# One hand-laid SBUF tile for two alternating transformer layers, and new orders of work at their seams

## The chip, the cores and the metric

The kernel runs on one core of a Trainium2 chip. The metric is device time in microseconds. The core has five engines with instruction streams of their own: TensorE (PE, with its weight loads shown apart as PEld), VectorE (DVE), ScalarE (ACT), GpSimd (POOL) and SyncE (SP); transfers are issued by SP, ACT or POOL and carried out by 16 DMA engines. On-chip data lie in SBUF, and PE writes its sums to PSUM.

## The reference

Four residual layers, A, B, A, B, over 2048 rows of 640 values in bfloat16. Both A layers have the same weights, and so have both B layers.

```python
x = x + A(layernorm(x));  x = x + B(layernorm(x))
x = x + A(layernorm(x));  x = x + B(layernorm(x))

def A(x, mem0, Wq, Wk, Wv, Wo, seg_len):      # 32 heads of 192, seg_len 32
    mem = mem0                                # 8 memory rows
    for s in range(64):
        h = concatenate([mem, x[32*s : 32*s+32]])
        q, k, v = h @ Wq, h @ Wk, h @ Wv      # per head
        p = softmax(where(mask, q @ k.T * scale, -1e9))
        o = (p @ v) @ Wo
        mem = o[:8]                           # the recurrence
        outs.append(o[8:])

def B(x, wqkv, w_phi, wo):                    # 32 heads of 20, linear attention
    q, k, v = split(x @ wqkv)
    phi_q = [softmax(q @ w_phi), softmax(-q @ w_phi)]
    phi_k = [softmax(k @ w_phi), softmax(-k @ w_phi)]
    kv, z = phi_k.T @ v, phi_k.sum(rows)
    return (phi_q @ kv) / (phi_q @ z + 1e-6) @ wo
```

Layer A is sequential: a segment needs the memory rows of the one before. The last 8 rows of every segment aren't needed by the next one, so the kernel computes them apart, in a preparation and a closing stage with large matmuls.

## The kernel before

A layer A consists of `A_pre` (queries, keys and values of the last 8 rows of every segment, in two halves of 32 segments and four rounds of 8 heads), `A_chain` (the recurrence) and `A_post` (the output product of those last rows). Weights of layer A stay in SBUF but for nine pieces, `wslot`, that are loaded anew in every segment, as is one part of `Wo`.

```python
with tc.tile_pool(name=f"A{li}_wres", bufs=1) as wres:
    big = wres.tile([P, NRES * PW], BF16, name="w_res")      # resident weights, rounds 3, 0, 1, 2
    slot = {(m, b): wres.tile([P, PW], BF16, name=f"wslot{m}{b}") for ...}
    wo_mid = wres.tile([P, 24 * 640], BF16, name="wo_mid")
    wo_end = wres.tile([P, 12 * 640], BF16, name="wo_end")
    ...
    self.A_pre(...)
    self.A_chain(...)
    self.A_post(at_dram, li, wo_mid, wo_end, big)
```

The closing stage, four blocks of 16 segments: tails are fetched, reordered by copies on DVE and ACT in turn, multiplied, and stored in 16 pieces.

```python
def A_post(self, at_dram, li, wo_mid, wo_end, big):
    ...
    for tb in range(NSEG // 16):
        o = 7680 + 12288 * (tb % 3)
        ot = big[:, o:o + 6144]...
        nc.sync.dma_start(out=ot, in_=self.otb_d[16 * tb:16 * tb + 16]...)
        ow = big[:, o + 6144:o + 12288]...
        for k in range(4):
            self.ev.copy(out=ow[:, 12 * k:12 * k + 12, :]..., in_=ot[:, :, 96 * k:96 * k + 96]...)
        for c in range(48):
            nc.tensor.matmul(p0[:, :], lhsT=ow[:, c, :], rhs=w[:, 0:512], ...)
            nc.tensor.matmul(p1[:, 0:128], lhsT=ow[:, c, :], rhs=w[:, 512:640], ...)
        ob = ...                                    # one copy on DVE, one on ACT
        for s in range(16):
            dq.next().dma_start(out=at_dram[row:row + 8, :], in_=ob[8 * s:8 * s + 8, :])
```

Layer B has pools of its own. It loads its weights and builds constants, then works in two phases over four groups of 512 rows.

```python
with tc.tile_pool(name=f"B{li}_w", bufs=1) as wp, ...:          # x2, wqkv, wo, wbd, osum, zm, expd, phi
    for j in (1, 2, 0):
        nc.scalar.dma_start(out=wqkv[:, :, D * j:D * j + D], in_=...)
    ...                                                        # constants on POOL: wbd, blk, mask, osum, expd

    def norm_T(g):                                             # four blocks of 128 rows
        for b in range(4 * g, 4 * g + 4):
            nc.sync.dma_start(out=xl[:], in_=x_dram[rows, :])
            nc.sync.dma_start(out=al[:], in_=at_dram[rows, :])
            nc.gpsimd.tensor_tensor(out=xt, in0=xl[:], in1=al[:], op=ALU.add)
            xn = self.ln_rows(bp, xt)
            ...                                                # five transposes, one copy on ACT

    for g in range(NG):                                        # first phase
        xnT = norm_T(g)
        keys_values(g, xnT)
        if waiting is not None:
            query_features(*waiting)
        waiting = (g, heads_T(xnT, 0, "qT"))
    query_features(*waiting)
    ...                                                        # kvm and zm from the sums
    for g in range(NG):                                        # second phase: divide, times wo, add x
        ...
        nc.sync.dma_start(out=xout_dram[rows, :], in_=ob[:])
        if xnext_dram is not None:
            xn = self.ln_rows(bp, ob)
            nc.sync.dma_start(out=xnext_dram[rows, :], in_=xn[:])
```

`A_pre` of the second layer A gathers its rows from the stored `xn` and loads the weights as it goes:

```python
for h in range(NH):                                            # two halves
    for k in range(NT):
        gather(xb, xn_dram, h, k)
        transpose_rows(xb, h, k)
    for ri, r in enumerate(...):                               # four rounds
        for mi, m in enumerate("KQ"):
            load_matrix(m, r)                                  # issued on SP
            ...                                                # 120 matmuls a round, copies to st
        nc.scalar.dma_start(out=self.kqb_d[...], in_=st)
        load_matrix("V", r)
        ...                                                    # 40 matmuls a round, copies, stores
```

Of the kernel before, what the change touches and what calls it, by code (L numbers as in the profile page):

```python
# [8 lines left out]
P = 128  # L9
# [9 lines left out]
LN_EPS = 1e-5  # L19

# [27 lines left out]
class RR:  # L48
# [5 lines left out]
    def next(self):  # L54
        x = self.items[self.i % len(self.items)]
        self.i += 1
        return x

# [42 lines left out]
class Kernel:  # L101
# [36 lines left out]

    def transp(self, out, in_, identity, tile_position=None):
        skip = out.base_partition() != 0  # L140
        if tile_position is None:
            tile_position = (in_.base_partition(), out.base_partition())
        return self.nc.tensor.matmul(out, in_, identity, is_transpose=True, tile_position=tile_position,
                                     skip_group_check=skip)

    def run(self, layers):
# [16 lines left out]
        self.dram = dram  # L163
        x_cur, attn, xn = self.A_x, None, None
        for li, Lt in enumerate(layers):
            last = li == len(layers) - 1
            if Lt == "A":
                if xn is None:
                    xn = dram.tile([S, Dm], BF16, name=f"xn{li}")[:]
                    if attn is not None:  # L170
                        self.layernorm(x_cur, xn, li, attn, xs[li - 1])
                        x_cur = xs[li - 1]
                attn = dram.tile([S, Dm], BF16, name=f"attn{li}")[:]
                self.layer_A(xn, attn, li, self.A_x if li == 0 else None)
                xn = None
            else:
# [3 lines left out]
                self.layer_B(x_cur, attn, x_next, xn, li)  # L180
                x_cur, attn = x_next, None
        if attn is not None:
            self.layernorm(x_cur, None, len(layers), attn, self.out)

    def ln_rows(self, lp, xt):
        m = self.ln_moments(lp, xt)
        return self.ln_apply(lp, xt, m, self.ln_deviation(lp, m))
# [23 lines left out]
    def ln_apply(self, lp, xt, mvr, sd16):  # L211
# [3 lines left out]
        xc = lp.tile([P, Dm], BF16, name="ln_xc")  # L215
        nc.vector.tensor_scalar(out=xc[:], in0=xt[:], scalar1=mvr[:, 0:1], scalar2=None, op0=ALU.subtract)
        xn = lp.tile([P, Dm], BF16, name="ln_xn")
        nc.vector.tensor_scalar(out=xn[:], in0=xc[:], scalar1=rstd[:], scalar2=None, op0=ALU.mult)
        return xn

    def layernorm(self, x_dram, xn_dram, li, add_dram=None, sum_dram=None):
        nc, tc, Dm = self.nc, self.tc, self.Dm
        with tc.tile_pool(name=f"ln{li}", bufs=3) as lp:
            dq = RR([nc.sync, nc.scalar])
            for b in range(self.NB):
                rows = slice(b * P, (b + 1) * P)
                xt = lp.tile([P, Dm], BF16, name="ln_x")
                dq.next().dma_start(out=xt[:], in_=x_dram[rows, :])
                if add_dram is not None:
                    at = lp.tile([P, Dm], BF16, name="ln_a")  # L230
                    dq.next().dma_start(out=at[:], in_=add_dram[rows, :])
                    xs = lp.tile([P, Dm], BF16, name="ln_s")
                    nc.vector.tensor_tensor(out=xs[:], in0=xt[:], in1=at[:], op=ALU.add)
                    dq.next().dma_start(out=sum_dram[rows, :], in_=xs[:])
                    xt = xs
                if xn_dram is not None:
                    xn = self.ln_rows(lp, xt)
                    dq.next().dma_start(out=xn_dram[rows, :], in_=xn[:])

    def layer_B(self, x_dram, at_dram, xout_dram, xnext_dram, li):  # L240
# [11 lines left out]
        with tc.tile_pool(name=f"B{li}_w", bufs=1) as wp, tc.tile_pool(name=f"B{li}_blk", bufs=3) as bp, \  # L252
                tc.tile_pool(name=f"B{li}_grp", bufs=2) as gp, \
                tc.tile_pool(name=f"B{li}_ps", bufs=3, space=bass.MemoryType.PSUM) as pp, \
                tc.tile_pool(name=f"B{li}_pt", bufs=2, space=bass.MemoryType.PSUM) as ptp, \
                tc.tile_pool(name=f"B{li}_kv", bufs=1, space=bass.MemoryType.PSUM) as kvp:
# [6 lines left out]
            x2 = wp.tile([P, NB, D], BF16, name="x2")  # L263
            wqkv = wp.tile([P, KC, 3 * D], BF16, name="wqkv")
            for j in (1, 2, 0):
                nc.scalar.dma_start(out=wqkv[:, :, D * j:D * j + D],
                                    in_=self.B_wqkv.rearrange("(k p) n -> p k n", p=P)[:, :, D * j:D * j + D])
            wo = wp.tile([P, NC_, D], BF16, name="b_wo")
            wbd = wp.tile([P, NC_, CH], BF16, name="wbd")
# [5 lines left out]
            blk = wp.tile([P, HC], BF16, name="blk")  # L275
# [5 lines left out]
            mask = wp.tile([P, HC, DH], BF16, name="bmask")  # L281
            nc.gpsimd.tensor_copy(out=mask[:], in_=bcast_last(blk[:], DH))

            osum = wp.tile([P, 2, NC_, P], BF16, name="osum")
            nc.gpsimd.memset(osum[:], 0.0)
            zm = wp.tile([P, 2, NC_, P], BF16, name="zm")
            nc.vector.memset(zm[:], 0.0)
            for sg in range(2):
                for c in range(NC_):
                    nh = sizes[c] // DH  # L290
                    o = osum[:, sg, c, :].rearrange("p (u h) -> p u h", u=2)[:, :, 32 * sg + HC * c:32 * sg + HC * c + nh]
# [787 lines left out]
```

The softmax here doesn't subtract the row's maximum and nothing guards it: scores larger than these inputs give would overflow.

## Time and profile before

| | |
|---|---|
| time, median of 3 | 3944.24 us (3936.85 to 3946.65) |
| span of the profiled execution | 3947.6 us, mean granted clock of TensorE 0.963 |
| busy PE, PEld | 3579.9 us (91%), 2253.8 us (57%) |
| busy DVE, ACT, POOL | 2363.6, 2042.9, 1611.7 us |
| DMA | 935.21 MB, mean 237 GB/s |

Stages by the trace, in us from the start of the span:

| stage | from | to |
|---|---|---|
| first layer A: preparation | 0 | 197 |
| its recurrence | 197 | 1607 and a last part of a segment |
| its closing product | 1629 | 1684 |
| first layer B: first phase | 1684 | 1897 |
| its second phase | 1897 | 1976 |
| second layer A: preparation | 1976 | 2166 |
| its recurrence | 2166 | 3588, nearly |
| its closing product | 3597 | 3651 |
| second layer B | 3651 | 3948 |

The busy shares are averages over stages with different limits, so a change at a seam is read from the windows around that seam. The columns of a table of windows are the length, the busy time of PE, PEld, DVE, ACT and POOL, the granted clock of PE as a share of full speed, the mean busy share of the DMA engines, and GB/s. The chain of waits follows the work that ended last back from the end: what stands in it was not hidden behind anything else. A busy PE isn't PE at its peak, since matmuls are pipelined and their ends are modelled.

### The profile page before, as it was taken

The page shows a single profiled execution, that of the slowest core. Times are in us where ns is not written, and L with a number is a line of the kernel's source. Part 1 is how long each engine was busy: PE and PEld are TensorE (multiplying, and loading weights), DVE is VectorE, ACT ScalarE, POOL GpSimd, SP SyncE. Part 2 cuts the span into 40 slices and gives each one's busy share as a digit, 9 for nine tenths or more (in the row PEclk, how much of TensorE's full clock was granted, in tenths as well). Part 3 has the DMA queues.
Part 4 walks back from the last instruction along what each step waited for, and adds up shares of the span by engine and source line. Part 5 has one row for each costly group of instructions (what it writes and reads, how often), then busy time and mean ns, then how long its engine had stood idle before and what let it go on. Part 6 is the DMA issues. An engine that isn't in the chain of part 4 may idle for free.

```text
span 3947.6 us, 168002 instructions
## 1 busy us (share of the span) xinstructions
PE 3579.9 (91%) x70296; PEld 2253.8 (57%) x70312; DVE 2363.6 (60%) x6102; ACT 2042.9 (52%) x5237; POOL 1611.7 (41%) x4303
## 2 busy tenths in 40 slices
PE   7889999999999999859879899999999999998598
PEld 6656655656666666535357565566556656555353
DVE  3556666666666666257633566666666666662574
ACT  2245655556656665335313565556555656563352
POOL 2445454545455554140022454455545554541400
PEclk9989999999999999979889899999999999999698
DMA  9888878888878887520187887888788878785200
GB/s 323 258 274 276 282 271 281 271 272 281 284 270 289 279 287 269 188 89 1 45 303 218 287 290 256 276 276 289 266 276 273 289 266 284 267 285 169 89 1 27
DMA packets 593411, 935.21 MB, mean 237 GB/s; under 512 B 148218, under 2 KB 409866, under 8 KB 592650
## 3 DMA queue, kind: packets, MB, share of 16 engines
q1 hardware_dynamic: 452042, 808.06, 59.1%
q0 software_dynamic: 65984, 81.08, 6.9%
q10 hardware_dynamic: 74624, 35.33, 3.3%
q8 instruction: 551, 9.03, 0.9%
q14 instruction: 210, 1.72, 0.1%
HBM read 855.97 MB, written 72.09 MB: 235 GB/s over the span
## 4 chain that ended last, share of the span: by engine, by line
PE 62%; DMA 16%; DVE 7%; ACT 6%; issue 5%; POOL 2%; SPq 0%; ACTq 0%; POOLq 0%; DVEq 0%
PE ps_qk L801 19%; DMA wo_end<-wo_rows 8%; PE ps_w L877 8%; PE ps_v L801 7%; PE ps_o L851 4%; PE ps_s L843 3%; PE ps_pre L705 3%; PE ps_s L904 2%; PE ps_qk L351 2%; PE pp L1036 2%; PE ps_s L838 2%; PE ps_wo L464 2%; DVE E L911 1%; ACT raw L811 1%; DMA kqb<-wo_mid 1%
## 5 line engine op out<-in xcount | busy, mean ns | idle before, releaser
L801 PEld LDWEIGHTS <-hT 128*32 128x32 bf16 x30720 | 747.7, 97 | 476.9 <-DVE hT L1011 60.4
L801 PE MATMUL ps_qk<-w_res,hT 128*32 128x384 bf16 x14336 | 770.6, 328 | 0.3
L811 ACT ACTIVATE raw<-ps_qk 128x384 bf16<-128x384 f32 x1024 | 503.1, 491 | 447.1 <-PE ps_s L904 249.1
L877 PEld LDWEIGHTS <-OT 128*32 128x32 bf16 x24576 | 437.5, 97 | 192.9 <-issue 96.5
L784 POOL DMA_DIRECT2D Vp<-vb x512 | 258.5, 505 | 684.8 <-PE ps_o L851 482.5
L816 DVE STREAM_TRANSPOSE KT<-raw 128x384 bf16<-128x384 bf16 x512 | 296.1, 578 | 198.2 <-ACT raw L811 194.2
L801 PE MATMUL ps_v<-w_res,hT 128*32 128x384 bf16 x7168 | 389.1, 329 | 1.7 <-issue 1.5
L819 DVE STREAM_TRANSPOSE QT<-raw 128x256 bf16<-128x256 bf16 x512 | 228.0, 445 | 270.0 <-ACT raw L811 241.3
L772 POOL DMA_DIRECT2D kqb<-kqb x512 | 291.0, 568 | 199.4 <-POOL KT L780 146.7
L832 DVE CAST Vp<-ps_v 64x384 bf16<-64x384 f32 x512 | 286.1, 559 | 107.6 <-ACT Vp L830 93.2
L870 POOL DMA_DIRECT2D otb<-otb x512 | 282.7, 552 | 161.1 <-DVE otb L866 119.5
L877 PE MATMUL ps_w<-wo_end,OT 128*32 128x160 bf16 x12288 | 286.3, 234 | 59.2 <-issue 33.1
L830 ACT ACTIVATE Vp<-ps_v 64x384 bf16<-64x384 f32 x512 | 246.3, 481 | 161.1 <-PE ps_v L801 125.9
L857 DVE CAST OT<-ps_o 128x192 bf16<-128x192 f32 x512 | 183.2, 358 | 227.4 <-PE ps_o L851 209.3
L851 PEld LDWEIGHTS <-Vp 80*128 80x128 bf16 x4096 | 183.1, 99 | 196.2 <-issue 133.1
L911 DVE TENSOR_TENSOR E<-E,ps_s 80x320 bf16<-80x320 bf16 x512 | 247.4, 483 | 73.6 <-ACT ps_s L910 68.8
L890 ACT ACTIVATE E<-ps_s 80x320 bf16<-80x320 f32 x512 | 221.9, 433 | 115.3 <-PE ps_s L843 102.9
L877 PE MATMUL ps_w<-wo_mid,OT 128*32 128x160 bf16 x12288 | 268.2, 235 | 12.9 <-issue 12.7
L851 PE MATMUL ps_o<-E,Vp 80*128 80x80 bf16 x4096 | 235.6, 202 | 34.4 <-issue 7.6
L843 PE MATMUL ps_s<-QT,KT 128*80 128x80 bf16 (+1 forms) x3072 | 234.6, 213 | 23.8 <-DVE KT L816 13.4
L856 ACT ACTIVATE OT<-ps_o 128x192 bf16<-128x192 f32 x512 | 167.8, 328 | 143.3 <-PE ps_o L851 143.3
L777 POOL COPY QT<-kqb 128x64 bf16<-128x64 bf16 x512 | 125.9, 246 | 283.8 <-PE ps_s L843 278.7
(152 smaller groups left out, 6173.3 us busy)
## 6 DMA issues: line engine op xcount, KB each, us to landing
wo_end<-wo_rows SPq DMA_DIRECT2D x780, 320.0 KB
wslotQ<-in_A_Wq_dram SPq DMA_DIRECT2D x402, 384.0 KB
wslotK<-in_A_Wk_dram SPq DMA_DIRECT2D x768, 192.0 KB
wslotV<-in_A_Wv_dram SPq DMA_DIRECT2D x768, 192.0 KB
kqb<-wo_mid ACTq DMA_DIRECT2D x16, 1536.0 KB
kqb<-kqb POOLq DMA_DIRECT2D x512, 48.0 KB, 5.0
vb<-wo_end POOLq DMA_DIRECT2D x128, 112.0 KB, 5.6
Vp<-vb POOLq DMA_DIRECT2D x512, 28.0 KB, 4.4
```

Source lines behind the costliest of these rows:

```text
L772: nc.gpsimd.dma_start(out=kqb[:], in_=self.kqb_d[s, :, r, :])
L784: nc.gpsimd.dma_start(out=Vs[n % 2][64:80, :], in_=self.vb_d[s, r].rearrange("g t f -> (g t) f"))
L801: nc.tensor.matmul(o[32 * g:32 * g + 32, 0:384], lhsT=hT[:, b, :], rhs=rhs, start=(i == 0), stop=(i == KC - 1), tile_position=(0, 32 * g), ...
L811: nc.scalar.activation(out=raw[:], in_=ps[:, 0:384], func=ACT.Copy)
L816: nc.vector.transpose(out=KT[:, :, 0:64], in_=raw[:, :].rearrange("p (c j) -> p c j", j=64))
L830: nc.scalar.activation(out=o, in_=i, func=ACT.Copy)
L832: nc.vector.tensor_copy(out=o, in_=i)
L843: nc.tensor.matmul(S[0:80, c0:c0 + 80 * (q1 - q0)], lhsT=KT[:, 3 * x + i, :], rhs=QT[:, x, q0:q1, :], start=False, stop=(x == 1 and i == 2 ...
L851: nc.tensor.matmul(O[x][:, 80 * i:80 * i + 80], lhsT=Vs[n % 2][0:80, 448 * x + k:448 * x + k + 128], rhs=E[0:80, 160 * x + 80 * e:160 * x ...
L870: nc.gpsimd.dma_start(out=self.otb_d[s, :, 96 * r:96 * r + 96], in_=otb[:, :, :].rearrange("p c t -> p (c t)"))
L877: nc.tensor.matmul(W[32 * g:32 * g + 32, 0:160], lhsT=OT[:, c, q:q + 32], rhs=w[:, 640 * i + 160 * g:640 * i + 160 * g + 160], start=(firs ...
L911: nc.vector.tensor_tensor(out=E[0:80, 0:320], in0=E[0:80, 0:320], in1=rc, op=ALU.mult)
```

## The change

All large buffers of both layers become views of one SBUF tile, at byte offsets that are chosen so that what a stage needs early lies on what the stage before gives up early. The tile is split at byte 64512. In layer A the lower part holds the weights of rounds 3 and 2, which the last segment uses first, the upper part those of round 0, the slots, those of round 1, and `Wo`. In layer B the lower part holds what is needed from the end of the first group on, the upper part weights and buffers of the first phase, then `x2`, and at the end `phi`.

```diff
+LATE = 64512
+ARENA = 202752
...
+        self.arena = arena.tile([P, ARENA // 2], BF16, name="arena")
...
-            for r in (3, 0, 1, 2):
-                for m in "KQV":
-                    for b in range(KC - (SLOTS[m] if r in (0, 3) else 0)):
-                        res[m, r, b] = big[:, at * PW:at * PW + PW]
+        low = self.view(0, LATE)
+        for r in (3, 2):
+            for m in "KQV":
+                for b in range(KC - (SLOTS[m] if r == 3 else 0)):
+                    res[m, r, b] = low[:, len(res) * PW:len(res) * PW + PW]
+        for m, r, b in [round 0] + [the slots] + [round 1]:
+            v = self.view(at, 2 * PW)
+            ...
+        wo_mid = self.view(at, 24 * 1280)
+        wo_end = self.view(at + 24 * 1280, 12 * 1280)
```

**Layer A's closing stage goes into layer B.** `A_post` becomes two functions, `fetch` and `multiply`, with two buffers for the tails and one store per block instead of 16. Layer B calls them between the steps of its first group. Constants that lie in the lower part come after the first group's keys and values.

```diff
+            with tc.issue_after(self.last_load.ins):
+                load_rows(0)
+            fetch, multiply = post
+            ow = [fetch(tb) for tb in range(2)]
+            for j in (1, 2, 0):
+                nc.sync.dma_start(out=wqkv[:, :, D * j:D * j + D], in_=...)
+            multiply(0, ow[0], kv_ps[0], side_bank("ps_post"))
+            ow.append(fetch(2))
+            rows = [norm_rows(b) for b in range(4)]
+            multiply(1, ow[1], kv_ps[1], side_bank("ps_post"))
+            ow.append(fetch(3))
+            multiply(2, ow[2], kv_ps[0], side_bank("ps_post"))
+            first_xnT = new_xnT()
+            for b in range(4):
+                turn_rows(b, rows[b], first_xnT)
+            multiply(3, ow[3], kv_ps[1], side_bank("ps_post"))
             for g in range(NG):
-                xnT = norm_T(g)
+                xnT = first_xnT if g == 0 else norm_T(g)
                 keys_values(g, xnT)
+                if g == 0:
+                    late_constants()          # osum, zm, expd, and the load of wo
...
-                for s in range(16):
-                    dq.next().dma_start(out=at_dram[row:row + 8, :], in_=ob[8 * s:8 * s + 8, :])
+            nc.sync.dma_start(out=av[16 * tb:16 * tb + 16, 24:32, :], in_=ob[:, :])
```

`last_load` is the last load of `Wo` in layer A; the first rows of `x` are asked for behind it on SP.

**The next weights are loaded beside layer B.** Layer B's second phase stores through POOL, which leaves SP's queue to the loads of layer A's preparation; only SP keeps the program's order there. The rows of the first half are gathered into buffers outside layer B's live data.

```diff
-                    nc.sync.dma_start(out=xout_dram[rows, :], in_=ob[:])
+                    nc.gpsimd.dma_start(out=xout_dram[rows, :], in_=ob[:])
...
-                        xn = self.ln_rows(bp, ob)
-                        nc.sync.dma_start(out=xnext_dram[rows, :], in_=xn[:])
+                        self.ln_rows(bp, ob, xn)
+                        nc.gpsimd.dma_start(out=xnext_dram[rows, :], in_=xn[:])
...
+                es.enter_context(tc.manual_schedule(engines={nc.sync.engine}))
+            if x_raw is None:
+                xB = [[self.view(LATE - 1280 * (i + 1), 1280) for i in range(2)], ...]
+                xT[0] = self.next_xT[:, :]
```

**Beside these**, the pools, PSUM among them, are given over tile by tile (`reuse_waits="tile"`) instead of as a whole, layer B adds the attention rows to `x2` in place, and the second step of the layernorm works in place:

```diff
-        nc.vector.tensor_scalar(out=xc[:], in0=xt[:], scalar1=mvr[:, 0:1], scalar2=None, op0=ALU.subtract)
-        nc.vector.tensor_scalar(out=xn[:], in0=xc[:], scalar1=rstd[:], scalar2=None, op0=ALU.mult)
+        nc.vector.tensor_scalar(out=xn, in0=xt[:], scalar1=mvr[:, 0:1], scalar2=None, op0=ALU.subtract)
+        nc.vector.tensor_scalar(out=xn, in0=xn, scalar1=rstd[:], scalar2=None, op0=ALU.mult)
```

## The prediction

> **What bounds the kernel now.** I read the page's busy shares and 40 slices first, then the chain of work that ended last (whole, and cut to the seams between stages), then a table of windows by stage, then the order of instructions at two seams.
>
> ```profile
> PE   7889999999999999859879899999999999998598
> PEclk9989999999999999979889899999999999999698
> DMA  9888878888878887520187887888788878785200
> ```
> Two long plateaus are the 64-segment recurrences of layers A; the dips between them are the seams that the change is about. There PE falls to 5, its granted clock to 6 or 7, and DMA from 8 to 0: PE waits for transfers in one place and the DMA engines stand still in the next.
>
> ```profile
> 197.00:1607.00 1410.00, 1334.86 (x32078) 842.65 (x32076) 917.86 (x2489) 836.83 (x2229) 702.85 (x1926) 0.99 0.82 278
> 1976.00:1994.00 18.00, 1.23 (x10) 1.10 (x11) 6.56 (x19) 1.61 (x5) 4.90 (x13) 0.51 0.64 211
> 1994.00:2066.00 72.00, 64.73 (x481) 48.81 (x481) 19.14 (x30) 16.25 (x30) 14.96 (x31) 0.91 0.93 322
> 2066.00:2166.00 100.00, 98.83 (x811) 78.89 (x810) 32.39 (x51) 28.79 (x52) 22.24 (x42) 1.00 0.76 229
> ```
> Columns: window, length, busy PE, weight load, DVE, ACT, POOL, clock, DMA share, GB/s. The recurrence (first row, 22.0 us per segment; the second layer A has 1404 us) holds 71% of the span and no operation of it changes. Rows two to four are the preparation of the second layer A: 18 us with 1.2 us of PE, 72 us at a DMA share of 0.93, then 100 us in which PE is full.
>
> ```profile
> 1684.29:1717.50 33.21, 3.06 (x23) 1.99 (x22) 15.63 (x33) 4.76 (x14) 27.15 (x48) 0.58 0.68 209
> 1717.50:1763.00 45.50, 35.19 (x180) 21.18 (x180) 32.60 (x72) 15.61 (x44) 14.95 (x31) 0.74 0.13 40
> 1802.00:1840.00 38.00, 35.18 (x231) 20.97 (x230) 26.55 (x49) 21.84 (x45) 1.87 (x4) 1.00 0.00 1
> 1896.65:1976.00 79.35, 69.11 (x306) 29.41 (x305) 56.47 (x149) 28.27 (x64) 6.38 (x30) 0.91 0.17 60
> ```
> Same columns, first layer B: after the closing product ends at 1684.3 come 33 us with 3 us of PE, a slow first group (45 us at clock 0.74), regular groups of 38 us, and an output phase of 79 us whose DMA share is 0.17. What fills the 33 us is in the chain:
>
> ```profile
> 1684.55 5.57 DMA wqkv<-in_B_wqkv_dram
> 1690.14 2.92 DMA attn<-obB
> 1693.09 2.19 DMA attn<-obB
> 1696.16 6.45 DMA B_al<-attn
> ```
> Weights, small stores, and the reload of the rows just stored, one behind the other, then the layernorm of four row blocks. At the other end of the closing product two instructions tell how it starts (brackets: idle before, and what ended it):
>
> ```profile
> 1615.15 0.72 PE L843 MATMUL ps_s<-QT,KT 128*80 128x80 bf16 x6 [5.73 <-DVE KT L816]
> 1629.32 0.61 PE L1036 MATMUL pp<-wo_end,w_res 128*128 128x512 bf16 x1 [5.71 <-DVE w_res L72]
> ```
> Even the last segment is held up: DVE had queued the closing stage's copy, which waited for its DMA, ahead of the transpose that the segment needed.
>
> **What the Trainium skill says.** "TensorE: Matmul & The Clock Gate", Part 1, What's actually happening: an idle array drops to half clock and needs sustained work to come back. The trace agrees: 0.51 to 0.74 behind each gap, 1.00 in steady groups; so filling a gap gains a little beyond it. "DMA: Bandwidth & Descriptors", Issuing engines are not separate DMA queues: transfers of all issuers interleave on the same 16 engines. So moving the output stores to POOL and the weights to SP only frees an issuing order; the gain must come from idle DMA time (share 0.00 in the regular groups). "SBUF — State Buffer", Who interferes with whom: DVE in its two-port modes and GpSimd lock each other out. The trace agrees:
>
> ```profile
> L216 DVE TENSOR_SCALAR ln_xc<-x,ln_mvr 128x640 bf16<-128x640 bf16 x10 | 13.1, 1307 | 0.3
> L216 DVE TENSOR_SCALAR ln_xc<-x,ln_mvr 128x640 bf16<-128x640 bf16 x6 | 2.1, 369 | 0.0
> ```
> The same subtraction takes 1307 ns between 1700 and 1730, beside the POOL additions, and 369 ns in the groups without them.
>
> **Part 1: closing product beside layer B's first group (twice).** The four products keep their 4 x 48 matmul pairs; 1629.0 to 1684.5 is 54.6 us of PE. What can move is behind them. From their end to the end of the first group's query projections: 1763.0 - 1684.3 = 78.7 us in the first layer B; in the other, 3651.4 to 3732.0 (where the chain's last query projections of that group end at 3731.9), 80.6 us. Afterwards the four row blocks are normalised and transposed between the products, and layer B's weights are asked for before the first product (the chain puts the last 5.6 us of their wait after it), so PE can go on with key projections. A regular group is 38 us but also contains the previous group's query features, 6 + 12 + 12 = 30 matmuls of 512 columns; the closely spaced ones start about 0.22 us apart, 6.5 us. So 38 - 6.5 = 31.5, and 4.5 for the waits on key copies and exponentials that a first group cannot fill: 36 us. Saving 78.7 - 36 = 42.7 and 80.6 - 36 = 44.6, together 87.
>
> Deductions. The 20 transposes move between the products: about 2 us a layer, 4. The constants (osum, expd, zm) may be written only after the last product, because they lie where its operands lie. On POOL they cost 4.1 (selects) + 1.6 (copies) + 1.4 + 1.3 (memsets) = 8.4 us, just when POOL should add the second group's rows (4 x 1.4) and DVE normalises; the first query features need them. I charge 3 us a layer, 6. Rest: 87 - 4 - 6 = **77 us**.
>
> The front. The new request order puts two 2 MB blocks of output weights and 0.65 MB of rows ahead of the first 1.57 MB of tails: about 6.2 MB, at the 360 GB/s of 1607 to 1629 some 17 us after 1604.5, so about 1622; its copies take 3 us more; the first product could start near 1625 instead of 1629.3. But if the copies are again ahead in DVE and ACT's order, the segment waits 8 us longer than now. I take 2 us of gain a layer, **4 us**. The 16 small stores per block becoming one are off the path behind the first three products and counted above behind the fourth.
>
> **Part 2: next weights beside layer B (once).** Preparation now takes 2166 - 1976 = 190 us. Its floor is PE: the chain shows regular rounds of 13.1 + 6.5 = 19.6 us, eight are 157, and 2 for the transposes: 159. Round 0's weights come to lie on parts of layer B that are dead after its first phase, so they and the first part of round 1 can be loaded in the output phase: about 24 pieces of 0.393 MB, 9.4 MB, or 33 us at 290 GB/s, of 79. The first four rounds then still need 36 pieces, 14.2 MB, and store 4 x (1.57 + 0.9) = 10 MB; 24.2 MB at the 322 GB/s seen there is 75 us against 78 of PE. Nearly balanced, so I leave 5 us of stalls and 2 us of start: 159 + 7 = 166, saving **24 us**. Its store wait (the chain shows 17.0 and 20.9 us for kqb out of wo_mid) shortens with the same pressure. The normalised rows for its first half come from groups 0 and 1, so the gather need not wait for the end.
>
> Off the path: in-place layernorm, renamed buffers, and POOL's issue of 32 stores at 0.5 to 0.6 us each. Sum: 77 + 4 + 24 = 105 us; 3944 - 105 = 3839. I shift it 4 us for full-clock matmuls at the seams not counted: **3835 us**.
>
> **Rivals.** (a) *The copy blocks the segment.* DVE and ACT run in order; if the tail copies stand early and the tails now land at 1622, the last segment ends 8 us later, twice, and the front is a loss of 16 instead of a gain of 4: 3855. For it: the line at 1615.15. Against: the whole of the wait may shift into time the product waited anyway.
> (b) *DMA is the bound.* In most segments the chain ends in a wait for wo_end of some 6.5 us, and preparation runs at 0.93. If the early weights only bring forward a queue that later rounds and stores fill again, Part 2 gives 10 us: 3849. Against it: 79 us at share 0.17 stand right before.
> (c) *One tile brings waits.* If dependencies inside the single tile are kept more coarsely than between separate tiles, slot loads in the recurrence start late. Just 0.5 us a segment over 128 segments is 64 us, which leaves 3899. Against it: the resident weights were regions of one tile already, and the nine slots, their sizes and their points of reloading stay.
> (d) *More overlap than I count.* The first matmuls of preparation could fill PE's 10 idle us of the output phase and the front could lose all its 12 us of idle time: 3805.
>
> **Range and chances.** (a) and (b) together give 3869, (d) 3805; some of (c) widens the upper side, so 3792 to 3878. Faster by over 2% means below 3865: 0.83. Within 2%: 0.14, mostly (a) with (b), or a weak (c). Slower by over 2%: 0.03, a strong (c) alone.
>
> **What would show it.** Right: after the closing product no PE gap over 5 us and a clock near 1; no B_al or wqkv wait in the chain there; DMA share above 0.4 in the output phase; preparation at 160 to 170 us; recurrences within 5 us of 1410 and 1404. Wrong: the gap before the closing product grows (a); preparation still shows waits for weights or kqb (b); segments longer than 22.0 us on average (c); first key projections waiting for POOL or the constants, which would make my 36 us too small. A recurrence that shifts by 2% would move the time by more than half of the whole sum, and would make the prediction wrong though each seam behaved as told.

## The result, and the profile after

The changed kernel takes 3853.14 us (median of 4 executions, 3847.97 to 3859.71) against 3945.44 us: a ratio of 0.977, 95% interval 0.975 to 0.980. The prediction was 3835 us, in a range of 3792 to 3878. So the kernel is faster by 92 us, and 17 us of the 109 expected are missing.

The slices of the page after: PE at the seams (slices 17 to 21 and the last three) no longer falls to 5 and its clock no longer to 6, and at the first seam (slices 18 to 20) DMA falls to 3, 0, 3 where it fell to 2, 0, 1.

```profile
PE   7889999999999999889899899999999999999897
PEclk9989999999999999989899899999999999999898
DMA  9888888778787888830376888787888888788100
```

The chain of waits of this execution follows only a small part of the span, so what comes now rests on windows and timelines. The windows of the first seam after (columns as before: length, busy PE, PEld, DVE, ACT, POOL, granted clock, DMA share, GB/s):

```profile
1653.00:1666.00 13.00, 13.00 (x102) 7.45 (x100) 8.20 (x23) 4.90 (x11) 3.68 (x11) 1.00 0.63 190
1666.00:1689.00 23.00, 15.35 (x114) 8.84 (x111) 12.19 (x41) 5.47 (x19) 14.37 (x24) 0.85 0.30 91
1689.00:1727.00 38.00, 30.67 (x178) 19.45 (x176) 19.71 (x39) 12.32 (x27) 14.28 (x27) 0.82 0.11 32
1838.00:1861.00 23.00, 17.27 (x54) 5.76 (x52) 16.07 (x55) 8.92 (x17) 0.00 (x0) 0.87 0.79 285
1861.00:1949.50 88.50, 73.93 (x317) 31.04 (x316) 60.51 (x158) 29.47 (x67) 23.94 (x65) 0.86 0.29 97
1949.50:1969.00 19.50, 19.31 (x148) 15.37 (x149) 6.51 (x13) 5.06 (x10) 3.70 (x9) 0.91 0.83 284
```

The 33 us with 3 us of PE are gone: the products end at 1689.0 and the key projections start there. But the last product's window has 23 us with 15.4 us of PE, the new loss at this place. In the fourth row the DMA engines work at 0.79 during the last stretch of layer B's first phase, where the kernel before moved nothing: the next layer's first weights. The last row is the first round of preparation, in which PE is full from its start.

Stage by stage, by the traces, in us. The two numbers of a cell are the first and the second seam; the last two rows exist once.

| | before | after | fourth bank (e1_bank) | all orders (e11_pool) |
|---|---|---|---|---|
| from the transpose that starts the last segment to the first product | 36.4, 36.6 | 29.7, 30.3 | 28.9, 29.6 | 30.4, 31.2 |
| four products | 55.1, 54.4 | 62.6, 63.5 | 53.1, 53.1 | 53.1, 53.1 |
| to the first key projection | 33.0, 33.5 | 0, 0 | 0, 0 | 0, 0 |
| first phase of layer B | 179.2, 181.3 | 172.1, 172.3 | 181.3, 182.1 | 171.8, 177.9 |
| output phase of layer B | 78.1, 78.1 | 84.5, 78.1 | 84.3, 78.1 | 81.3, 79.4 |
| preparation of the second layer A, to the first matmul of its recurrence | 191.5 | 164.2 | 164.2 | 163.6 |
| last matmul to the end | 3.4 | 9.9 | 9.9 | 3.4 |

Every column is one traced execution. The two recurrences together, from the first transpose of the memory rows to the last, have 2709 us before and 2700 after. No experiment below edits them, and they lie between 2697 and 2723 us there; so I read all differences without them. The two traced spans differ by 101.4 us, of which the recurrences are 9.3. The rest went from 1238.4 to 1146.3 us, which is 92.1, near the medians' 92.3, though these hold the recurrences. Its parts are: products, gap and first phase -32.7 and -33.5; front -6.7 and -6.3; preparation -27.3; output phase +6.4; end +6.5; all else +1.5.

**The front**, the table's first row. PE's instructions around the end of the last segment, after:

```profile
1619.30 0.73 PE L908 MATMUL ps_s<-QT,KT 128*80 128x80 bf16 x6 [6.20 <-DVE KT L881]
...
1626.56 0.38 PE L1102 MATMUL kv<-arena 128*128 128x512 bf16 x1
```

The segment is still held up by a copy that stands ahead of its transpose (6.2 us, before 5.7; at the second seam 6.5, before 7.1). But the first product now follows 7.3 us later without a wait, where before it needed 14.2 us, the last 5.7 of them for a DVE copy that started only at 1628.70. SP's queue shows when the tails are asked for, before and then after:

```profile
1604.05 0.38 SPq L1025 DMA_DIRECT2D w_res<-otb  x1
1604.53 7.17 SPq L553 DMA_DIRECT2D wo_end<-wo_rows  x6
1611.75 5.84 SPq L553 DMA_DIRECT2D w_res<-wo_rows  x6
1618.15 13.79 SPq L1025 DMA_DIRECT2D w_res<-otb  x3
```

```profile
1608.50 0.38 SPq L1090 DMA_DIRECT2D arena<-otb  x1
1608.98 12.71 SPq L608 DMA_DIRECT2D arena<-wo_rows  x12
1622.19 2.85 SPq L348 DMA_DIRECT2D arena<-in_A_x_dram  x4
1625.57 0.38 SPq L1090 DMA_DIRECT2D arena<-otb  x1
```

The first block's tails stand ahead of the output weights in SP's order in both kernels. What held the first product back before, by the profile, were copies of the *second* block's tails, asked for at 1618.15:

```profile
1628.70 1.03 DVE L72 COPY w_res<-w_res 128x1536 bf16<-128x1536 bf16 x2 [6.68 <-DMA w_res<-otb]
```

After, those tails are asked for at 1625.57 and copied from 1635.99, long behind the start of the first product. So it isn't that they come earlier: the first product no longer depends on them.

**The new gap.** Three engines around 1670, each a view of its own: PE, then ACT, then POOL.

```profile
1674.55 0.69 PE L163 MATMUL ps_x<-ident,arena 128*128 128x128 bf16 x5 [7.66 <-ACT arena L86]
```

```profile
1670.25 0.29 ACT L231 ACTIVATE ln_lv<-ln_mvr,eps 128x1 f32<-128x1 f32 x1 [7.44 <-POOL ln_mvr L224]
...
1673.80 2.48 ACT L86 ACTIVATE arena<-ps_x 128x640 bf16<-128x640 bf16 x4
```

```profile
1665.76 4.09 POOL L354 TENSOR_TENSOR arena<-arena 128x640 bf16<-128x640 bf16 x3 [3.51 <-DMA arena<-attn]
```

The transposes of the first group's rows go to three PSUM banks; the fourth needs one that ACT has copied out. ACT has those copies behind the layernorm of the *second* group's rows, which waits for POOL, and POOL for the second product's stored rows, stored at 1659.85 and asked for again at 1662.59. So a row block that nobody needs yet holds up the product that everybody waits for: 7.7 us without PE at both seams, and then, at this one, matmuls of 0.63 us instead of 0.38 until 1677.

### The profile page after: what moved, and what is told of

The parts are those of the page before. It is cut to its first block, busy times and chain, and to the rows that moved or that the text cites. A ratio compares the mean times of both kernels' runs of the same rounds, so it can differ in the third digit from the quotient of the medians.

```text
span 3846.2 us, 167810 instructions
## 1 busy us (share of the span) xinstructions
PE 3563.9 (93%) x70312; PEld 2245.0 (58%) x70312; DVE 2348.3 (61%) x6102; ACT 2038.6 (53%) x5237; POOL 1638.9 (43%) x4351
## 5 line engine op out<-in xcount | busy, mean ns | idle before, releaser
L866 PE MATMUL ps_qk<-arena,hT 128*32 128x384 bf16 x20480 | 1005.0, 329 | 31.1 <-DMA arena<-in_A_Wk_dram 8.7
L942 PE MATMUL ps_w<-arena,OT 128*32 128x160 bf16 x24576 | 552.8, 235 | 66.6 <-issue 38.3
L942 PEld LDWEIGHTS <-OT 128*32 128x32 bf16 x24576 | 437.0, 97 | 186.0 <-issue 92.3
L866 PE MATMUL ps_v<-arena,hT 128*32 128x384 bf16 x10240 | 538.7, 330 | 0.5 <-issue 0.2
L916 PE MATMUL ps_o<-E,Vp 80*128 80x80 bf16 x4096 | 235.2, 202 | 32.7 <-DMA Vp<-vb 5.7
L949 PE MATMUL ps_idle<-arena,ident 128*128 128x384 bf16 x1024 | 234.0, 330 | 4.8 <-issue 4.8
```

The lines of the kernel that those rows point to most:

```text
L866: nc.tensor.matmul(o[32 * g:32 * g + 32, 0:384], lhsT=hT[:, b, :], rhs=rhs, start=(i == 0), stop=(i == KC - 1), tile_position=(0, 32 * g), ...
L916: nc.tensor.matmul(O[x][:, 80 * i:80 * i + 80], lhsT=Vs[n % 2][0:80, 448 * x + k:448 * x + k + 128], rhs=E[0:80, 160 * x + 80 * e:160 * x ...
L942: nc.tensor.matmul(W[32 * g:32 * g + 32, 0:160], lhsT=OT[:, c, q:q + 32], rhs=w[:, 640 * i + 160 * g:640 * i + 160 * g + 160], start=(firs ...
```

## The experiments

All are edits of the changed kernel, and an experiment's stages come from one traced execution. "Sum" is products, gap and first phase of one seam: 267.3 and 269.2 before, 234.6 and 235.7 after.

**e1_bank: one more bank for the fourth row block.**

```diff
-                pt = bank("ps_x", BF16)
+                pt = kv_ps[2][:, :].bitcast(BF16) if b == 3 else bank("ps_x", BF16)
```

> The changed kernel, with the fourth row block of each layer B's first group transposed into a PSUM bank of its own. Theory: the 7.7 us for which PE stands between the third and the fourth closing product come from ACT's order: the copies that free the banks stand behind layernorm steps of the second group, which still wait for rows. Then PE no longer waits there, the four products end 7 to 9 us earlier in each layer, and the whole is 14 to 18 us shorter. Rival: the fourth block's rows aren't normalised in time; then the gap stays at 7 us or more and the time doesn't move.

3847.42 us, ratio 0.976 (0.973 to 0.979): 5.7 us below the kernel after, not 14 to 18. Products 53.1 us at both seams, 9.5 and 10.4 less: the gap's cause is right. But the first phase grows by 9.2 and 9.9, and the sum stays (234.3, 235.1). PE and then ACT behind the products show where it goes:

```profile
1683.13 5.02 PE L382 MATMUL ps_qk<-arena 128*120 128x512 bf16 x15 [4.52 <-ACT arena L86]
```

```profile
1679.88 0.29 ACT L231 ACTIVATE ln_lv<-ln_mvr,eps 128x1 f32<-128x1 f32 x1 [7.19 <-POOL ln_mvr L224]
```

It is the same pattern one step later: ACT has a layernorm step that waits 7.2 us for POOL ahead of the copies of the first keys; a DVE wait of 3.5 us follows at 1697.7. The gain turned into new waits, and the next experiments on this seam ask what orders would keep it.

**e2_tail: last stores of the kernel on SP instead of POOL.**

```diff
-                    nc.gpsimd.dma_start(out=xout_dram[rows, :], in_=ob[:])
+                    (nc.sync if xnext_dram is None else nc.gpsimd).dma_start(out=xout_dram[rows, :], in_=ob[:])
```

> The changed kernel, with the stores of the last layer's second phase issued on SP again, all others as they are. Theory: stores through POOL make the end of the program 6.5 us later after the last sum (9.9 us instead of 3.4); the span ends 3 to 4 us after the last sum and the whole is 6 us shorter. Rival: the end belongs to something else of the new layout (the larger pool that is closed there); then the 9.9 us stay.

3841.92 us, ratio 0.974 (0.971 to 0.977). From the last matmul to the end 3.4 us instead of 9.9. The end of POOL's stream after, and of SP's queue here:

```profile
3837.11 0.54 POOL L517 DMA_DIRECT2D out_dram<-arena  x1 [1.51 <-DVE arena L515]
```

```profile
3826.68 6.48 SPq L517 DMA_DIRECT2D out_dram<-arena  x4
```

The stores wait for the same additions on DVE and land after 2.1 and 1.8 us (median), but the spans end at 3846.2 and 3835.6, which is 9.1 us behind the start of the last issue in one and 2.4 us behind the end of the last issue in the other. The end of this program costs 6.5 us more when its last store is GpSimd's. The medians differ by 11.2: in the trace, the recurrences are 3.0 us shorter and the first output phase 2.7, neither of which the edit touches.

**e3_act: all stores of the second phase on ACT.**

```diff
-                    nc.gpsimd.dma_start(out=xout_dram[rows, :], in_=ob[:])
+                    nc.scalar.dma_start(out=xout_dram[rows, :], in_=ob[:])
...                   (the stores of xn likewise)
```

> The changed kernel, with all stores of both layers' second phases issued on ACT instead of POOL. Theory: POOL, which now waits for each row block to issue its stores, delays the casts of the layernorm, and so DVE and the reciprocal that PE waits for (1.4 us before, 2.0 to 2.6 now); on ACT the first layer B's second phase falls from 84 to about 78 us, and the end from 9.9 to about 4 us: 12 us shorter together, with the preparation of the second layer A unchanged at 164. Rival 1: the loads of the next weights slow it; then the second phase stays at 84. Rival 2: ACT, which then waits for the same rows, takes POOL's place and the phase is as long or longer.

3844.11 us, ratio 0.975 (0.972 to 0.979). The end is back at 3.4 us and the first output phase at 80.8 us instead of 84.5, still 2.7 above the kernel before, so the 78 of my theory don't come. In five kernels with POOL's stores (e2_tail, e4_behind, e5_pool, e6_undo, e8_edge) it takes 81.3 to 81.8: against those, ACT is better by 0.5 to 1.0 us, and the second rival is nearer.

**e4_behind: the tail copies queued behind the last segment.**

```diff
-            ow = [fetch(tb) for tb in range(2)]
+            with tc.issue_after(self.last_dve.ins), tc.issue_after(self.last_act.ins):
+                ow = [fetch(tb) for tb in range(2)]
```

> The changed kernel, with the first two sets of tail copies queued behind the last instructions of the recurrence on DVE and ACT. Theory: the 6.2 to 6.5 us for which the last segment waits are the copies at the head of the two queues; then the last segment has no such wait, the first product starts 3 to 5 us earlier than now, 6 to 10 us over both layers. Rival: the tails land so late that the product waits for them instead; then the segment's wait goes, but the first product starts when it does now, and the time stays.

3854.75 us, ratio 0.977 (0.974 to 0.981). The last segment's wait is gone (6.2 and 6.5 to 0.0), but the first product starts only 2.1 us earlier at each seam, and the products take 1.3 and 1.8 us longer, in part since their first matmuls run at 0.63 us instead of 0.38. What takes its place is in the last segment's own output product:

```profile
1621.03 0.32 PE L943 MATMUL ps_w<-arena,OT 128*32 128x160 bf16 x8 [0.52 <-DMA arena<-wo_rows]
1622.01 0.32 PE L943 MATMUL ps_w<-arena,OT 128*32 128x160 bf16 x8 [0.67 <-DMA arena<-wo_rows]
```

At this seam it waits five times, 3.2 us in sum, for pieces of `Wo` that are still being loaded; the wait of 6.2 us had hidden that. Removing the copy's wait brings nothing.

**e5_pool: layer B's PSUM handed over as a whole, as before.**

```diff
-        with tc.tile_pool(name=f"B{li}_kv", bufs=1, space=bass.MemoryType.PSUM, reuse_waits="tile") as kvp, \
+        with tc.tile_pool(name=f"B{li}_kv", bufs=1, space=bass.MemoryType.PSUM) as kvp, \
...                   (and the two other PSUM pools)
```

> The changed kernel, with layer B's three PSUM pools given over as wholes again instead of tile by tile. Theory: the 5.7 and 6.2 us for which the first product waited for DVE in the kernel before, though its own copies were done 10 us earlier, were the handing over of PSUM as a whole: then the first product again starts 13 to 15 us after the last segment's own wait instead of 7 to 8, and the time grows by 8 to 14 us over both layers. Rival: the gain at that place comes from the requests' new order; then nothing changes.

3853.86 us, ratio 0.978 (0.975 to 0.980), the front 30.8 and 29.3 us: no change. The front's gain doesn't come from how layer B's PSUM is handed over. Nor does it come from the rival's order of requests, since the second tails are asked for later than before. The other pools' handover and the single tile weren't taken back.

**e6_undo: the first group's rows only after the four products.**

```diff
-            rows = [norm_rows(b) for b in range(4)]
...
+            last = multiply(3, ow[3], kv_ps[1], side_bank("ps_post"))
+            with tc.issue_after(last.ins):
+                rows = [norm_rows(b) for b in range(4)]
             first_xnT = new_xnT()
             for b in range(4):
                 turn_rows(b, rows[b], first_xnT)
-            multiply(3, ow[3], kv_ps[1], side_bank("ps_post"))
```

> The changed kernel, with the loads and layernorms of the first group's rows put behind the store of the last product instead of between the products. What it takes back is the overlap alone; layer B's weights are loaded before. Theory: the four products shrink to 53 to 55 us, and 22 to 30 us of waiting come back between them and the first keys (33 before, without the 5.6 us of weights), so that products, gap and first phase together are 13 to 22 us a layer longer than now, 26 to 44 over both. Rival: the gain of the change is the early load of the weights and the single store; then the growth is below 15.

3882.59 us, ratio 0.985 (0.983 to 0.987). Products 52.3 us, then a gap of 25.5 us, sums 255.1 and 258.1: 20.5 and 22.4 us above the kernel after. By the stages, this is what the overlap is worth (42.9 in sum, expected 26 to 44; the medians, with the recurrences in them, differ by 29); the other 12 and 11 us of the seam's gain I put down to the earlier weights and the single stores, which no run tests apart.

**e7_nopre: second-phase stores on SP, meant to hold back the next weights.**

```diff
-                    nc.gpsimd.dma_start(out=xout_dram[rows, :], in_=ob[:])
-                        nc.gpsimd.dma_start(out=xnext_dram[rows, :], in_=xn[:])
+                    nc.sync.dma_start(out=xout_dram[rows, :], in_=ob[:])
+                        nc.sync.dma_start(out=xnext_dram[rows, :], in_=xn[:])
```

> The changed kernel, with the stores of both layers' second phases on SP as before, so that the loads of the next weights stand behind them in SP's queue: no weights beside the second phase. Theory: the second layer A's preparation goes from 164 back to 183 to 191 us, the first layer B's second phase from 81 to 84 back to 78, the end from 9.9 to 3.4 after the last sum: 8 to 18 us longer in all. Rival: preparation is bound by its own stores and later loads; then it rises by less than 12 and the whole is no longer or shorter. If the second phase stays above 81 here, neither POOL nor the loads make it longer.

3841.35 us, ratio 0.975 (0.973 to 0.977). The preparation stays at 163.6 us. The edit misses its aim: the first round's weights stand ahead of the stores in SP's order and are loaded at 1831 to 1854, before the first store. So it tells only that the stores don't need POOL for the early loads, and it gains the 6.5 us of the end and 3.0 of the output phase. e10_late is the test that this one was to be.

**e8_edge: e1_bank, and each later group's layernorm behind the key copies of the group before.**

```diff
+                    with tc.issue_after(self.k_copy["s"]), tc.issue_after(self.k_copy["v"]):
+                        xn = norm_rows(b)
```

(`k_copy` holds the last copies of keys out of PSUM, "s" on ACT and "v" on DVE)

> The kernel with the fourth transposition bank, and with the layernorms of later groups queued on ACT and DVE behind the key copies of the group before. In the kernel with the bank alone the products ended 9.5 and 10.4 us earlier, but the first phase grew by 9.2 and 9.9. Theory: what gave it back is the same head of the line one step later: on ACT the layernorm of the third group's rows, which wait for the third product's store, stands ahead of the copies of the first keys. Then with the edges the products stay at 53 us and the first phase is at 172 us or below: 16 to 20 us less than the changed kernel over both layers. Rival: the first phase is bound by POOL, on which the constants that may come only after the last product stand ahead of the second group's additions; then it stays at 180 or more, and the sum as it was.

3857.11 us, ratio 0.979 (0.977 to 0.982). The waits of e1_bank for ACT and DVE disappear, yet the first phase takes 184.7 and 185.6 us, the sums 237.9 and 238.8. PE idles 29 of 186 us, as in e1_bank (28 of 181; after, 21 of 172), but in small waits, none over 2.8 us. The theory falls, and the first phase is above 180, as the rival about POOL had it; e11_pool tests that one.

**e9_order: the same more gently, two groups apart.**

```diff
+                        if g >= 2:
+                            es.enter_context(tc.issue_after(self.k_copy["s"][5 * (g - 1) - 1]))
+                        if g == 3:
+                            es.enter_context(tc.issue_after(self.k_copy["v"][1]))
```

(with the fourth bank of e1_bank and the stores of e7_nopre; `k_copy` now lists all the copies)

> The kernel after with a fourth PSUM bank for the last row block's transposes, second-phase stores on SP, and an order on ACT and DVE: the layernorm of group 2 and of group 3 queues behind the key copies of the groups two before, not ahead of the first keys. Theory (in-order engines: early layernorm instructions stand at the head of ACT and DVE and hold copies back): products near 53 us a layer as with the fourth bank alone, and the first phase back to 172 to 176 us, since the waits of 4.5 and 3.5 us behind the first keys are gone; the sum of both 225 to 229 us a layer, 6 to 10 below the kernel after. Rival (the rows' layernorm takes its time from the same stretch wherever it is queued): products near 53 but a first phase of 181 us or more, the sum 234 to 238.

3843.11 us, ratio 0.974 (0.972 to 0.976). Products 53.4, first phase 185.1 and 185.4: ACT's and DVE's order alone was not the cause, and my theory falls as stated. The trace names the third engine, PE and then POOL:

```profile
1697.08 0.37 PE L431 MATMUL kv<-arena 128*120 128x126 bf16 x2 [7.86 <-POOL arena L417]
```

```profile
1682.82 1.38 POOL L311 MEMSET arena<- 128x1536 bf16 x1
...
1691.19 5.43 POOL L354 TENSOR_TENSOR arena<-arena 128x640 bf16<-128x640 bf16 x4
1696.57 0.74 POOL L417 CAST arena<-rk 128x64 bf16<-128x64 f32 x2
```

From 1682.8 to 1696.6 POOL writes the late constants (8.3 us) and adds the third group's rows (5.4 us); the small copy that the first sum of keys and values needs stands behind both. In the kernel after this batch runs from 1687.6 to 1701.4; PE arrives at 1701.3 and waits 1.1 us there, so next to nothing of it is seen: the longer products hid it.

**e11_pool: e9_order, and POOL in order too.**

```diff
+                    self.rk_copy.append(nc.gpsimd.tensor_copy(out=vr[:, :, :, DH], in_=rk[:]).ins)
...
+                            es.enter_context(tc.issue_after(self.rk_copy[4 * (g - 1) - 1]))     # g >= 2
...
-                    late_constants()
+                    with tc.issue_after(self.rk_copy[3]):
+                        late_constants()
```

> The kernel of e9_order with GpSimd put in order as well: the constants that are written after the last product, and the additions of the rows of groups 2 and 3, queue behind the copies of the reciprocals for the keys of the group two before. Theory (with the products 9 us shorter, the first group's keys and values meet GpSimd's batch of 8.3 us of constants and 5.4 us of additions, which stands ahead of those copies: the trace of e9_order shows TensorE waiting 7.9 us there and then running at a clock of 0.71): products 53 us, first phase 170 to 176 us, the sum of both 223 to 229 us a layer against 234.7 in the kernel after and 238.5 in e9_order, and a time 18 to 30 us below that of e9_order. Rival (the work only meets the groups later, and its place is no matter): the 7.9 us disappear, other waits grow, and the sum stays at 234 us or more.

3825.97 us, ratio 0.968 (0.965 to 0.972): the best version, outside the interval of the kernel after. The windows of its products and of its first group, which compare with the second and third row above:

```profile
1629.00:1682.00 53.00, 52.63 (x397) 30.47 (x402) 20.49 (x58) 15.54 (x31) 14.49 (x25) 1.00 0.72 224
1682.00:1720.00 38.00, 29.76 (x199) 19.05 (x197) 20.26 (x38) 14.24 (x32) 15.83 (x30) 0.96 0.14 40
```

The products are full at clock 1.00, and the group behind them keeps 0.96 instead of 0.82. From its first key projection to the end of its queries it takes 33.4 us (34.8 at the second seam), after 38.2 and 38.5; PE's wait for POOL is gone. The sums are 224.8 and 230.9: -13.7 and -7.9 against e9_order, so the first seam is within what I expected and the second 2 us above it; the whole gains 17.1 us on e9_order, just under the 18 expected. At the second seam the last stretch of the first phase, from the last group's query features on, ran at a clock of 0.60 instead of 0.83 and took 3.4 us longer (22.5 against 19.1); why, no run tells.

**e12b_const: e1_bank with the stores on SP, and only the constants behind the first copies.**

```diff
-                    late_constants()
+                    with tc.issue_after(self.rk_copy[3]):
+                        late_constants()
```

> The kernel after with the fourth PSUM bank for the last block's transposes, second-phase stores on SP, and only the constants (8.3 us on GpSimd) queued behind the first group's copies of the reciprocals; the layernorm of the later groups keeps its own order. If the constants are the cost: sum of products and first phase 226 to 230 us a layer. If the layernorm of the next rows is the cost (the 4.5 and 3.5 us for ACT and DVE in e1_bank): the sum stays at 232 to 236 us. If both share it, 229 to 232.

3840.88 us, ratio 0.973 (0.970 to 0.976). Sums 231.7 and 232.0: both share it. The constants alone bring 2.6 and 3.2 us against e1_bank, and the wait of 3.5 us for DVE is down to 0.7, but the key projections still wait 4.2 us for ACT. The rows' order on the three engines brings the other 6.9 and 1.1.

**e10_late: stores on SP, and the next weights behind the last of them.**

```diff
-                        load_matrix(m, r)
+                        with (tc.issue_after(self.last_store.ins) if x_raw is None and turn == 1 and mi == 0 else ExitStack()):
+                            load_matrix(m, r)
```

> The kernel after with second-phase stores on SP and the loads of the preparation's first round queued behind the last of those stores, so that no weight of the next layer A is loaded beside layer B. Theory (the preparation's 27 us come from loading beside layer B): the preparation takes 183 to 191 us instead of 164, the time rises by 19 to 27 against the variant with the stores on SP alone, and the output phase before it goes from 81.5 back to about 78 if the loads cause its 3.4 us. Rival (DMA queues only move, the gain comes from gathering rows early and from the shared tile): the preparation stays under 176 us and the rise is below 12 us.

3868.64 us, ratio 0.981 (0.980 to 0.983). The preparation takes 185.4 us, 21.8 more than in e7_nopre (the medians differ by 27.3, expected 19 to 27); the early loads are the larger part of its gain, and the rival falls. Last stretch of the first phase and start of the preparation:

```profile
1833.00:1856.00 23.00, 17.03 (x54) 5.84 (x53) 16.11 (x56) 8.93 (x17) 0.00 (x0) 0.87 0.00 1
...
1960.00:2040.00 80.00, 72.10 (x538) 54.02 (x537) 22.08 (x35) 18.98 (x35) 12.66 (x24) 0.94 0.94 322
```

The 0.79 of the kernel after is 0.00 here, and the 80 us are again at a DMA share of 0.94 with 8 us of PE missing. Against the kernel before (191.5), 6.1 us of gain remain without early loads; I put them down to rows that are gathered earlier, which no run tests by itself.

**The output phase.** This run has 78.6 us there, which looks as if the loads caused the 3.4 us. They don't: e9_order and e12b_const keep the loads and have 78.8 us. The first and third group after, and then in e12b_const:

```profile
1861.20:1884.30 23.10, 20.02 (x69) 7.41 (x69) 10.42 (x23) 5.80 (x11) 2.23 (x6) 0.69 0.17 59
...
1905.70:1926.40 20.70, 18.11 (x82) 7.63 (x81) 15.30 (x42) 7.39 (x17) 7.88 (x21) 0.92 0.35 112
```

```profile
1868.90:1889.40 20.50, 17.43 (x69) 6.92 (x68) 10.28 (x24) 6.18 (x13) 0.74 (x4) 0.80 0.17 59
...
1910.40:1928.90 18.50, 16.54 (x82) 7.23 (x81) 15.01 (x43) 7.28 (x17) 3.49 (x13) 1.00 0.40 118
```

Groups two to four are 3.0 us longer in sum where POOL issues the stores (61.3 against 58.3; e7_nopre also has 58.3). It isn't POOL alone: with the stores on ACT (e3_act) they take 60.9. So the short groups belong to stores on SP; why, no run tells. In the last layer, which has half as many stores and no layernorm behind them, the phase takes 77.8 to 78.1 us with POOL and 77.5 to 79.4 without. The first group's 2.6 us go with a clock of 0.69 instead of 0.80; e1_bank, e7_nopre and e11_pool have them as well, and e2_tail, where POOL stores and the weights are loaded, has not (20.5 us). What sets that clock stays open; with one trace of each kernel it may differ between executions too.

## Why the prediction was right, and where its sum was off

The verdict and the range hold, and the two mechanisms are shown: e6_undo takes the overlap away and loses 20 to 22 us a seam, e10_late takes the early loads away and loses 22 us.

- **Part 1, predicted 77, measured 66.3** (products, gap and first phase together). The first group takes 38.2 and 38.5 us from its first key projection to the end of its queries, not 36: 4.7 of the missing 10.7. Another 6.6 are the deductions, "about 2 us a layer" for transposes and "3 us a layer" for constants: the products grew by 7.5 and 9.1 us instead (later groups return 0.6). Of PE's time the transposes cost under 1 us (53.1 us of products with the fourth bank, 52.3 in e6_undo without them); the rest is a wait for a PSUM bank behind ACT's early layernorm. The step that missed is charging moved work by PE's instructions alone, without asking what stands ahead of it on the engine that empties its bank. With the orders mended (e11_pool) this part brings 42.6 and 38.4 us, 81 in all: the 77 were there. The sign I gave for a 36 that is too small, first keys that wait for POOL or the constants, is all but absent after (1.1 us) and shows only in e9_order (7.9 us).
- **The constants.** I charged 3 us a layer for POOL's 8.4 us. In the kernel after they cost at most the 1.1 us, as PE arrives late; with the fourth bank they cost 2.6 and 3.2. The size was right for the kernel with the fourth bank.
- **The front, predicted 4, measured 13.0.** The step "the new request order puts two 2 MB blocks of output weights and 0.65 MB of rows ahead of the first 1.57 MB of tails" is false: the tails are asked for first, at 1608.5, as they were before, and copied at 1618.1. The gain is that the first product no longer waits for the copies of the second block's tails, 5.7 and 6.2 us before. e5_pool excludes the handover of layer B's PSUM, and the later request excludes its order; what made the first product depend on those copies stays open.
- **Part 2, predicted 24, measured 27.3.** The bytes were near (9.4 MB predicted; 23 us at 285 GB/s are 6.6, and the output phase moves 3 to 4 MB more than before or in e10_late), their place was not: 20 of the 26 early loads are issued in the first phase, 15 of these from 1842.4 on, when the last matmul that reads wqkv has ended (1842.1). So the share above 0.4 in the output phase that I named as a sign didn't appear (0.29), though its effect did.
- **POOL's stores, booked as off the path, cost 6.5 us at the end** (e2_tail) **and about 3 in the output phase** (the groups compared above); most of the rest there goes with the clock. The prediction counts 32 stores, those of the first layer B; the 16 of the last layer, with which the program ends, are in none of its terms. The profile before has no output store on POOL and could have told neither size.
- **Full clock at the seams, predicted 4.** It can't be told apart from the terms above; the first group still ran at 0.82.

In sum: 109 - 10.7 (part 1) + 9.0 (front) + 3.3 (part 2) - 12.9 (stores and output phase) - 4 (clock) - 1.5 (all else) = 92.2. That the total came so near is in part luck: 12.3 us too little and 29.1 too much met in it.

Of the rivals, (a) keeps a grain: the copy still blocks the segment by 6 us, but not by 8 more, and e4_behind shows that this costs nothing. (b) falls with e10_late and the early window. (c) falls: the recurrences are not longer in sum. (d) came half true at the front: of its 12 us of idle time a layer, one wait of about 6 is gone and the other stays. The sign "no PE gap over 5 us after the closing product" was met to the letter, while a gap of 7.7 us stood inside the product, where the sign did not reach. The sign "recurrences within 5 us" was missed: they went from 1350.5 and 1358.6 us to 1354.3 and 1345.6, and the kernels of the experiments scatter as much.

## What to carry to other kernels

When work is moved beside a full PE, follow each moved piece through the instruction order of the engines that feed it and empty its banks: a piece for later that stands ahead of a copy for now stops PE as surely as a missing bank. Take a wait away from PE and look again at once, because the next engine's batch that it had hidden (here POOL's 13.7 us) comes to light; only ordering ACT, DVE and POOL together kept the gain, 9.8 us at the first seam and 4.8 at the second. And try a program's last stores on more than one queue: here SP or ACT ended 6.5 us sooner than POOL.

## What the runs showed of the hardware beyond that

- This program ends 9.9 us after its last matmul if the last stores are issued by GpSimd (kernel after), 3.4 us if by SyncE (e2_tail) or ScalarE (e3_act), with the same landing time of about 2 us.
- In the first layer B's output phase, groups two to four take 58.3 us in sum with the stores issued by SyncE, 60.9 by ScalarE and 61.3 by GpSimd.
- The two recurrences, untouched, differ by up to 26 us in sum (1%) between kernels.
